# Attention in halves of the heads, a hand-ordered first group, and unread products on TensorE

## The chip, the cores and the metric

One core of a Trainium2 chip. The metric is device microseconds (us) of one execution; a median is over the executions of a kernel that were timed. The trace's span (first to last instruction) is 1.8 to 2.2 us shorter than the timed figure. All runs told of here are in the fast state. Times inside a kernel are us from the span's start.

Some words used throughout: a *turn* is a transposition on TensorE; *kv*, *q_t*, *product* and *turn* are the steps of attention, and a *leftover* step does the same for the 64 leftover tokens of two batches; the *chain* is the work followed back from the last instruction, at each step to what released it; the *granted clock* is the share of full speed that TensorE was allowed, and half rate is 0.5.

## The reference, cut to what matters

```python
# q, k, v: (8, 8, 576, 64) fp32
kv  = einsum('bhsd,bhse->bhde', k, v)
out = einsum('bhsd,bhde->bhse', q, kv)
out = out / sqrt(mean(out*out, -1) + 1e-6) * g_norm
x = out as (4608, 512)                 # tokens by heads*dim
y = ((x @ w1) * (x @ w2) @ w3) @ w_out # d_ff 1024, weights in fp64
```

The kernel folds w3 and w_out into one matrix (`w3o`, the fold stage), and works on nine groups T of 512 tokens: one for 512 tokens of each of the 8 batches, and a last one (`x_left`) for the 64 leftover tokens of all batches. A group has a gate stage (x @ w1, x @ w2 and their product, 8 column blocks f) and a projection by `w3o`. The attention of batch T+1 is put in pieces between the gate blocks of group T. The weights arrive as 8 byte words, 512 KB for a piece, and are converted to fp32 on ScalarE and VectorE.

## The kernel before

```python
w1_sb = const.tile([P, NP, DF], FP32, name="w1_sb")     # 128 x 4 x 1024
w2_sb = const.tile([P, NP, DF], FP32, name="w2_sb")

def load_raw(src):                      # 512 KB of 8 byte words
    raw = fold.tile([P, c, n], src.dtype, name="raw", bufs=4)
    nc.sync.dma_start(out=raw, in_=src)

def convert(dst, raw):                  # ScalarE: low, abs; VectorE: four steps
    nc.scalar.activation(low, lo, AF.Copy, ...)              # L116
    nc.scalar.activation(dst, hi.bitcast(FP32), AF.Abs)      # L117
    nc.vector.tensor_scalar(out=dst, ...)                    # L118
    nc.vector.tensor_scalar(out=dst_bits, ...)               # L121
    nc.vector.scalar_tensor_tensor(out=low_bits, in0=hi, ..) # L124, last to read raw
    nc.vector.tensor_tensor(out=dst_bits, ..., op=ALU.add)   # L128

def gate(T, f):
    cols = slice(f * P, (f + 1) * P)
    for w_sb in (w1_sb, w2_sb):
        g_ps = bank(ps_mm, "mm")
        for c in range(NP):
            nc.tensor.matmul(g_ps, lhsT=w_sb[:, c, cols], rhs=xT[T][:, c, :], ...)
    nc.scalar.copy(a_sb, prods[0])
    nc.vector.tensor_mul(ab[T, f], a_sb, prods[1])
# ... (cut: kv, q_t, product, norm, turn of attention)
# first group
load_batch(0)
for f, piece in enumerate(attention(0)):
    raws = [load_raw(gate_src(w, f)) for w in (w1, w2)]
    for w_sb, raw in zip((w1_sb, w2_sb), raws):
        convert(w_sb[:, :, f * P:(f + 1) * P], raw)
    piece()
# ... (cut)
for T in range(NG):
    pieces = attention(T + 1) if T + 1 < B else []
    late = 3 if T == 0 else 0
    for f in range(KF):
        gate(T, f)
        due = max(f + 1 - late, 0) * len(pieces) // (KF - late)
        # T == 0: load and convert part f of w_out; then run pieces[done:due]
    # T == 0: turn w3 and fold it with w_out
    project(T)
```

TensorE's order is the program's; that of the other engines is chosen by a scheduler.

## Time and profile before

| | before |
|---|---|
| median | 971.7 us (3 runs, 970.5 to 972.5) |
| span of the profiled run | 969.7 us |
| first gate in full swing | 64.0 |
| first fold block | 144.3 |
| project(0) starts | 206.2 |
| after that | 763.5 us with no wait of TensorE |

The page, the waits, the stretches and the chain are shown and read in the prediction below. One thing that it passed over is in the timeline of TensorE before (start us, duration us, engine, line, operation, tile written <- read, shapes, count, idle before and its releaser):

```profile
49.93 2.08 PE L292 MATMUL mm<-xT,w_sb 128*128 128x512 f32 x2 [0.78 <-ACT xT L263]
64.00 6.16 PE L292 MATMUL mm<-xT,w_sb 128*128 128x512 f32 x8 [11.99 <-DVE w_sb L128]
```

The first gate issues two instructions (one of its eight products; an fp32 product is two instructions), stands 12 us and then goes on. Its own column block had been converted by then: with a tile of its own this gate runs through from 49.2 (before_wtiles, below). What it stood for is the subject of half of the experiments.

### The profile page before, as it was taken

How to read it: one execution, taken by the hardware profiler on the slowest of the kernel's cores; microseconds unless marked ns; L12 is line 12 of the kernel's file. 1: busy time of each engine (PE TensorE's matmuls, PEld its weight loads, DVE VectorE, ACT ScalarE, POOL GpSimd, SP SyncE). 2: the span in 40 equal slices, each digit the busy share in tenths (PEclk: the TensorE clock that was granted, in tenths of full speed). 3: DMA queues.
4: the chain of work that ended last, by engine and by line, in shares of the span. 5: the costliest groups of instructions: out<-in, count | busy, mean ns of one | idle time of the engine just before them, and what ended most of it. 6: DMA issues, size and time to landing. Idle time of an engine off the chain costs nothing.

```text
span 969.7 us, 7839 instructions
## 1 busy us (share of the span) xinstructions
PE 915.6 (94%) x3232; PEld 455.6 (47%) x3232; DVE 223.8 (23%) x421; ACT 182.1 (19%) x332; POOL 0.7 (0%) x6
## 2 busy tenths in 40 slices
PE   4249979999999999999999999999999999999998
PEld 4214554444554455445544554554455544444443
DVE  2986256600120122112201220122012200000010
ACT  2663243300121022102200220122012200000000
POOL 0000000000000000000000000000000000000000
PEclk9659999999999999999999999999999999999999
DMA  8984413100310131013003200310000000000001
GB/s 233 279 276 156 141 55 130 44 11 33 98 44 19 36 96 45 22 53 93 18 22 98 65 12 22 112 51 1 32 11 1 1 33 11 0 22 22 1 0 43
DMA packets 54980, 59.23 MB, mean 61 GB/s; under 512 B 14496, under 2 KB 47264, under 8 KB 54944
## 3 DMA queue, kind: packets, MB, share of 16 engines
q1 hardware_dynamic: 54944, 58.73, 19.7%
q8 instruction: 25, 0.41, 0.2%
q14 instruction: 11, 0.09, 0.0%
HBM read 49.28 MB, written 9.44 MB: 61 GB/s over the span
## 4 chain that ended last, share of the span: by engine, by line
PE 93%; DVE 3%; DMA 2%; ACT 1%; issue 1%; SPq 0%; DVEq 0%; ACTq 0%
PE mm L292 51%; PE mm L344 25%; PE mm L333 6%; PE at L163 3%; PE at L223 3%; PE at L258 1%; PE at L180 1%; DMA v_sb<-in_v_dram 1%; DMA raw<-in_moe_w_dram 1%; DVE low L124 1%; PE mm L316 1%; DVE w_sb L128 1%; PE at L244 1%; ACT low L116 0%; DVE w_sb L118 0%
## 5 line engine op out<-in xcount | busy, mean ns | idle before, releaser
L292 PE MATMUL mm<-xT,w_sb 128*128 128x512 f32 x1024 | 453.2, 597 | 12.8 <-DVE w_sb L128 12.0
L292 PEld LDWEIGHTS mm<-xT,w_sb 128*128 128x128 f32 x1024 | 191.9, 191 | 238.9 <-issue 223.0
L344 PE MATMUL mm<-w3o_sb,ab 128*128 128x512 f32 x576 | 248.7, 592 | 0.0
L344 PEld LDWEIGHTS mm<-w3o_sb,ab 128*128 128x128 f32 x576 | 109.0, 190 | 134.9 <-issue 134.7
L303 DVE TENSOR_TENSOR ab<-a_sb,mm 128x512 f32<-128x512 f32 x72 | 49.5, 688 | 435.9 <-PE mm L292 435.9
L301 ACT COPY a_sb<-mm 128x512 f32<-128x512 f32 x72 | 42.2, 586 | 275.5 <-PE mm L292 275.5
L352 ACT COPY o_sb<-mm 128x512 f32<-128x512 f32 x18 | 10.5, 586 | 256.2 <-PE mm L344 256.2
L333 PE MATMUL mm<-wo_sb,w3T 128*128 128x512 f32 x128 | 57.7, 606 | 0.0
L292 PE MATMUL mm<-x_left,w_sb 128*128 128x512 f32 x128 | 55.1, 592 | 0.0
L354 DVE COPY o_sb<-mm 128x512 f32<-128x512 f32 x18 | 12.5, 692 | 176.4 <-PE mm L344 176.4
L258 PE MATMUL at<-ident,xn 128*128 128x128 f32 x144 | 23.7, 293 | 20.6 <-DVE xn L210 20.6
L223 PEld LDWEIGHTS at<-kv_bd,qT 128*128 128x128 f32 x256 | 34.8, 200 | 15.0 <-issue 12.4
L200 ACT ACTIVATE sq<-at 128x512 f32<-128x512 f32 (+1 forms) x40 | 22.1, 551 | 102.0 <-PE at L223 101.0
L292 PEld LDWEIGHTS mm<-x_left,w_sb 128*128 128x128 f32 x128 | 24.3, 190 | 30.6 <-issue 30.6
L333 PEld LDWEIGHTS mm<-wo_sb,w3T 128*128 128x128 f32 x128 | 24.5, 196 | 28.3 <-issue 28.0
L223 PE MATMUL at<-kv_bd,qT 128*128 128x128 f32 x256 | 35.9, 286 | 1.6 <-DVE xn L210 1.0
L163 PE MATMUL at<-v_sb,k_sb 128*64 128x64 f32 x512 | 23.7, 240 | 11.6 <-DMA v_sb<-in_v_dram 11.6
L202 DVE TENSOR_REDUCE inv<-sq 128x8 f32<-128x512 f32 (+1 forms) x40 | 25.3, 632 | 30.5 <-ACT sq L200 30.5
L258 PEld LDWEIGHTS at<-ident,xn 128*128 128x128 f32 x144 | 18.3, 150 | 28.8 <-DVE xn L210 12.2
L116 ACT ACTIVATE low<-raw 128x512 f32<-128x512 uint32 x40 | 27.0, 676 | 20.7 <-DVE w_sb L128 17.8
L263 ACT ACTIVATE xT<-at,g_col 128x512 f32<-128x512 f32 x32 | 21.9, 685 | 47.7 <-PE at L258 47.7
L124 DVE SCALAR_TENSOR_TENSOR low<-raw,low 128x512 uint32<-128x512 uint32 x40 | 27.1, 687 | 7.5 <-ACT low L116 6.9
(39 smaller groups left out, 295.4 us busy)
## 6 DMA issues: line engine op xcount, KB each, us to landing
raw<-in_moe_w_dram SPq DMA_DIRECT2D x32, 512.0 KB, 4.5
k_sb<-in_k_dram SPq DMA_DIRECT2D x8, 1024.0 KB, 6.0
v_sb<-in_v_dram SPq DMA_DIRECT2D x8, 1024.0 KB, 8.9
q_sb<-in_q_dram SPq DMA_DIRECT2D x8, 1024.0 KB, 5.3
out_dram<-o_sb SPq DMA_DIRECT2D x32, 256.0 KB, 2.3
raw<-in_moe_w_out_dram SPq DMA_DIRECT2D x8, 512.0 KB, 4.1
kl_sb<-in_k_dram SPq DMA_DIRECT2D x8, 128.0 KB, 6.2
vl_sb<-in_v_dram SPq DMA_DIRECT2D x8, 128.0 KB, 8.8
```

The costliest lines, as they stand in the source:

```text
L116: nc.scalar.activation(low, lo, AF.Copy, scale=2.0 ** -51, bias=2.0)
L124: nc.vector.scalar_tensor_tensor(out=low_bits, in0=hi, scalar=0x80000000, in1=low_bits, op0=ALU.bitwise_and, op1=ALU.bitwise_or,)
L163: nc.tensor.matmul(kv_ps[e * D:(e + 1) * D, r, :], lhsT=k_sb[:, h, cols] if j < J else kl_sb[:, h, :], rhs=v_sb[:, h, cols] if j < J else ...
L200: nc.scalar.activation(sq[:, cols], o_ps[:, cols], AF.Square)
L202: nc.vector.tensor_reduce(out=inv, in_=sq[:, cols].rearrange("p (h d) -> p h d", d=D), axis=AX.X, op=ALU.add,)
L223: nc.tensor.matmul(o_ps[:, h * P:(h + 1) * P], lhsT=qT[i, half][:, h, :], rhs=bd[:, half * HB + h, :], start=True, stop=True,)
L258: nc.tensor.transpose(t_ps[:, r, :], xn[:, 2 * r:2 * r + 2, :], ident)
L292: nc.tensor.matmul(g_ps, lhsT=w_sb[:, c, cols], rhs=xT[T][:, c, :], start=(c == 0), stop=(c == NP - 1),)
L301: nc.scalar.copy(a_sb, prods[0])
L303: nc.vector.tensor_mul(ab[T, f], a_sb, prods[1])
L333: nc.tensor.matmul(f_ps, lhsT=t[:, j, :], rhs=wo_sb[:, j, :], start=(j == 0), stop=(j == KF - 1))
L344: nc.tensor.matmul(o_ps, lhsT=ab[T, f][:, m * P:(m + 1) * P], rhs=w3o_sb[:, f, :], start=(f == 0), stop=(f == KF - 1),)
```

## The change

Its intent: start TensorE earlier. Batch 0 is loaded and worked on in two halves of the heads; the first group's work on ScalarE, VectorE and the load queue is put in program order, with the weights of gate f+2 converted before gate f; w_out and the first w3 pieces ride along; batch 1's attention moves into the fold stage; and 24 products that nobody reads keep TensorE's clock up in the early waits. The core of the diff:

```diff
-    def load_batch(b):
+    def load_half(b, half):            # k, kl, v, vl, q of four heads
+        heads = slice(half * HB, (half + 1) * HB)
...
+        pieces = []
+        for half in range(2):
+            pieces += [
+                [(kv, half), (q_t, 0, half)],
+                [(product, 0, half), (q_t, 1, half)],
+                [(product, 1, half), (turn, 0, half)],
+                [(turn, 1, half)],
+            ]
+        if b % 2:
+            pieces[6] += [(q_t_left,)]
+            pieces[7] += [(product_left,)]
+            pieces += [[(turn_left,)]]
...
+    def keep_warm(n):
+        t = bank(ps_mm, "mm")
+        for _ in range(n):
+            nc.tensor.matmul(t[:, 0:P], lhsT=ident, rhs=ident, start=True, stop=True)
...
+        keep_warm(16)
+        for name in ("kv0", "q_t00", "q_t10", "product00", "product10"):
+            first[name]()
+        keep_warm(4)
+        # ... second half, convert_gates(0), keep_warm(4), turns, convert_gates(1)
+        for f in range(KF):
+            wo_raw = load_wo(f)
+            if f + 2 < KF:
+                raws = load_gates(f + 2)
+                convert_gates(f + 2, raws)
+            else:
+                i = f + 2 - KF
+                w3_sb[i] = convert_w3(load_w3(i))
+            convert(wo_sb[:, f:f + 1, :], wo_raw)
+            gate(0, f)
+            if f in (3, 5):
+                load_half(1, f // 4)
...
+    for i in range(KF):                # fold stage, with batch 1's pieces
+        ...
+        pieces[i]()
+        fold_block(i)
+    pieces[KF]()
...
+    for T in range(1, NG):
+        # ...
+            due = (f + 1) * len(pieces) // KF
```

Also: copies of kv split between VectorE and ScalarE, one buffer fewer for `ab` and `o_sb` each, and one more for `qT`. In the changed kernel the conversion's lines are L130, L131 (ScalarE) and L132, L135, L138, L142 (VectorE), the gate's matmul is L322 and its product L333, the w3 turn L351, the fold L368, the projection L379, the leftover product L256, its transpose L282, the unread products L412.

> **What bounds the kernel now.** I read the page's busy shares and slices first, to see which engine is the limit and where it isn't.
>
> ```profile
> PE 915.6 (94%) x3232; PEld 455.6 (47%) x3232; DVE 223.8 (23%) x421; ACT 182.1 (19%) x332; POOL 0.7 (0%) x6
> ...
> PE   4249979999999999999999999999999999999998
> ...
> PEclk9659999999999999999999999999999999999999
> ```
>
> TensorE is the limit, and every hole in it lies in the first six slices of 24.2 us. Nothing can be won after 145 us, only lost. The waits of TensorE over the whole span say the same (engine, line, what it waited for, us in total, times, longest):
>
> ```profile
> PE at L258 <- DVE xn L210: 20.6, 4, 8.9
> PE mm L292 <- DVE w_sb L128: 12.0, 1, 12.0
> PE at L163 <- DMA v_sb<-in_v_dram: 11.6, 1, 11.6
> ...
> ```
>
> So: 11.6 us until batch 0 has landed; 20.6 us of transposes waiting for a norm; 12.0 us of the first gate waiting for converted weights. Asked for the waits after 206 us, the trace has none by a matmul. Busy times by stretch then show how bad the start is (us, busy time and count of PE, PEld, DVE, ACT, POOL, then granted clock, DMA share, GB/s):
>
> ```profile
> 40.00:50.00 10.00, 1.61 (x7) 1.21 (x7) 7.53 (x16) 4.03 (x7) 0.00 (x0) 0.50 1.12 285
> 50.00:60.00 10.00, 2.01 (x2) 0.43 (x2) 6.84 (x14) 5.00 (x9) 0.00 (x0) 0.50 0.95 302
> 130.00:140.00 10.00, 7.55 (x58) 5.50 (x56) 3.41 (x9) 3.87 (x8) 0.00 (x0) 0.86 0.00 1
> 140.00:150.00 10.00, 7.06 (x19) 3.50 (x19) 8.72 (x17) 5.71 (x9) 0.00 (x0) 0.80 0.63 211
> ```
>
> Last, the chain that ended last gives the stages (start us, us, what):
>
> ```profile
> 64.00 29.34 PE mm L292 x62
> ...
> 132.80 0.91 PE at L244 x19
> ...
> 136.74 0.43 DVE xn L210
> 137.31 1.09 PE at L258 x4
> ...
> 206.24 18.88 PE mm L344 x44
> ```
>
> The gates of group 0 run steadily from 64.0, batch 1's attention is spread among them, the fold of w3 with w_out takes over at 138, and project(0) begins at 206.2. From there 763.5 us of dense TensorE work remain. The change can win in the 206 us before that point. The middle lines show a cost I need below: the leftover product (L244) is followed at once by its own transpose (L258), and TensorE stands for the norm between them.
>
> **What the Trainium skill says.** (1) "TensorE: Matmul & The Clock Gate", Part 1: The HAM clock gate: the array is half-rate by default and a free-running window of 3413 ns decides. The trace agrees: from windows of 0.5 and 1 us the clock falls at 28.0, 137.25 and 144.1; 109.2 us is 32 such windows, 6.85 is two. (2) Same page, "Why this matters for your kernels": no idle gaps over some 3 us. Here 2.45 us (134.85 to 137.31) was enough, and the clock was half until 140.6. (3) Same page, "Architectural detail": ScalarE and VectorE are strict FIFO. That matters as the change fixes their program order. (4) "DMA: Bandwidth & Descriptors", "Anatomy of one DMA": about 2.0 us fixed plus the bytes, stated for another descriptor path. Here a 512 KB piece takes at least 3.0 us to land (last row of the next fences), so a load issued only when its data are due costs about that much.
>
> **The change part by part.**
>
> *Unit costs.* A gate block is 16 matmul instructions in 6.87 us (chain rows "6.87 PE mm L292 x16"); a fold block the same; one w3 turn of a row block 0.87; batch 1's attention: 3.51 kv, 1.76 q transposes, 3.56 products, 0.44 + 1.5 leftovers, 1.76 + 0.44 turns, 13 us. A conversion, from the timeline (start us, us, ...):
>
> ```profile
> 59.80 0.42 DVE L118 TENSOR_SCALAR w_sb<-w_sb 128x512 f32<-128x512 f32 x1
> 60.25 0.43 DVE L121 TENSOR_SCALAR w_sb<-w_sb 128x512 uint32<-128x512 uint32 x1
> 60.62 0.69 DVE L124 SCALAR_TENSOR_TENSOR low<-raw,low 128x512 uint32<-128x512 uint32 x1
> 61.23 0.68 DVE L128 CUSTOM_DVE_ANT_0 w_sb<-w_sb,low 128x1024 uint16<-128x1024 uint16 x1
> 61.83 0.42 DVE L118 TENSOR_SCALAR w_sb<-w_sb 128x512 f32<-128x512 f32 x1
> ```
>
> and the loads of such pieces, from the view of that buffer:
>
> ```profile
> DMA to landing us min/median/max: 3.0/4.4/8.7
> ```
>
> That is 2.0 us of VectorE per raw piece of 512 KB, after 1.35 us of ScalarE (L116, L117); the raw buffer is free when L124 ends, 1.44 us into it.
>
> *Start, by halves.* The first kv needs 1.18 MB in place of 2.36. At the 0.29 MB/us of the first 20 us, from 1.9 us, plus the 2 us by which the old landing (11.5) exceeds that reckoning: 7.9 us. The unread products (32 instructions) warm the array before. Half 1's v lands near 13.3. Following the norm through ScalarE and VectorE in order (square 0.6, sum 0.69, root 0.3, reciprocal 0.2, product 0.69) the last norm ends near 23; the four gate pieces 0 and 1 convert at 23.3 to 31.3. The first gate starts near 27 rather than 64.
>
> *Gate stage.* Per block VectorE has three conversions and one product, 3 x 2.0 + 0.65 = 6.7 us, against 6.87 of TensorE, which looks balanced. But the raw ring has still 4 buffers, and pieces are now loaded in the order w_out(f), gate a(f+2), gate b(f+2) and converted a, b, w_out. Numbering the loads, a(f+2) takes the buffer of w_out(f-1), the last converted before it, and is itself the next due. So every block pays a whole load: 3.2 us landing (estimate from the 3.0 minimum) + 1.35 ScalarE + 2.0 + 2.0 + 1.44 until w_out releases its buffer = 10.0 us. Block 0 releases at 31.4 + 5.44 = 36.8; seven more give 107; the two halves of batch 1 pushed into the queue at f = 3 and 5 (1.77 MB each, 6 us) add about 1 each: 109, and 110 with the last L128. TensorE's gates (6.87 of 10 us) hide under this, cold or not.
>
> *Fold stage.* The first fold needs all of w_out, hence the 110, and turn 1 and the first attention piece at half clock (some 5 us from 107.8) make it 112.5. Then 8 x 6.87 + 6 x 0.87 + 10.5 of attention = 70.7. The old wait for the leftover norm is gone here, a fold block lies between. project(0) starts near 184 instead of 206.2: 22 us won, of a possible 43 if the gate stage ran at TensorE's pace.
>
> *The later groups.* Odd batches now have nine pieces over eight gates, so (f+1) x 9 // 8 gives seven pieces by f = 6 and two after f = 7: turn and leftover product, and at once the leftover turn. Before, a gate lay between:
>
> ```profile
> 385.72 1.47 PE at L244 x32
> 387.19 7.06 PE mm L292 x16
> 394.26 0.87 PE at L258 x8
> ```
>
> In groups 2, 4 and 6 (batches 3, 5, 7) TensorE therefore stands as it did at 134: leftover product from 132.73 to 134.27, turn at 137.31, 3.0 us. The clock probably falls for one window: half of 3.4 is 1.7, times a chance I put at 0.7 from how the gap falls across windows: 1.2. Three times 4.2 = 12.7 us lost. The copies of kv moved to ScalarE, a smaller o_sb and ab ring and the split turns lie under 6.87 us gates and cost nothing.
>
> *Sum:* 969.7 - 22 + 12.7 = 960 of span, and 1.8 for the usual difference to the timed figure: **962 us**, 1.0% faster.
>
> **The rivals.** *A: the ring doesn't stall.* If loads run far enough ahead, the gate stage is 8 x 6.9 and fold starts some 22 us earlier: 940. For it: VectorE and DMA have the throughput (285 to 302 GB/s above, 12.6 MB + 3.5 in 55 us). Against: four buffers and this order. *B: the leftover wait is short or filled.* Then about 950 with the stall, 928 without. Against: 3.0 us measured in the same situation. *C: the start is DMA bound.* The stage needs 16 MB, 55 us at 0.29 MB/us; as each block also waits, more contention than my 2 us could make the stage 10 us longer: 972. *D: halves stall the later groups,* as loads of T+2 wait for halves of T+1. Against: 12 us of loads, and 27 us of project(T) plus the last gates to hide them in; I give it nothing.
>
> **Range and chances.** The sum has eight times the uncertainty of a load's latency (0.5 us each: 4 us), 3 us in the start, 4 us in the leftover waits. Around 962 that is some 6 us; A and B give a tail below. 80%: 944 to 970. Over 2% faster is under 952.3: both stalls as sized, 0.70, with a 0.04 chance of it; only the ring, 0.12 at half; only the leftovers, 0.13 at 0.9; neither, 0.05: together 0.26. Slower by 2%: 0.02. Within: 0.72.
>
> **What would show it.** First kv near 8 and first gate near 27. Gate stage: conversions in bursts of three with a VectorE hole of about 3 us each 10 us, put down to the raw load; with period near 7 the ring step is wrong. First fold near 112, project(0) near 184. In groups 2, 4 and 6, about 3 us of transpose waiting for xn each; none anywhere else after project(0). If idle of TensorE appears in odd groups at their start, D is right; if project(0) starts before 170 or the leftover waits are under 1 us, the prediction is too slow.

## The result, and the profile after

968.6 us median of 4 runs (967.75 to 969.64) against 972.0 (970.5 to 972.54) of the kernel before on the same chip. The ratio is 0.9968, 95% interval 0.9951 to 0.9985. Ratios here are the mean time of one kernel's fast runs over that of the kernel before in the same rounds, so they are not quite the ratio of the medians quoted. The gain is 0.3%, where 1.0% was forecast.

The changed kernel's page (busy time and share; then the slices, now of 24.1 us):

```profile
PE 927.7 (96%) x3280; PEld 460.0 (48%) x3280; DVE 222.1 (23%) x421; ACT 189.8 (20%) x364; POOL 0.7 (0%) x6
...
PE   8588999999999998999999989999999899999998
...
PEclk9789999999999998999999989999999899999999
```

The first slices are far fuller. But there are three new dents, in slices 16, 24 and 32, in both PE and clock: they come every two groups. TensorE's waits in it:

```profile
PE mm L322 <- DVE w_sb L142: 18.7, 7, 6.4
PE at L282 <- DVE xn L226: 8.9, 3, 3.0
PE at L271 <- DVE xn L226: 1.4, 1, 1.4
```

The wait for batch 0 has gone from 11.6 us to 0.2 beside the unread products, and that for norms at the start from 20.6 to some 2. The gates still wait 18.7 us for conversions. The leftover transposes (L282) wait three times 3.0. The chain that ended last, at the stages that matter:

```profile
36.00 8.39 PE mm L322 x14
44.48 0.69 DVE ab L333
45.17 0.35 DVE w_sb L132
...
46.60 0.70 DVE w_sb L142
47.35 6.29 PE mm L322 x14
...
113.52 6.87 PE mm L368 x16
...
184.79 27.47 PE mm L379 x64
```

Project(0) starts at 184.8, where 184 was forecast: 21.4 us won (206.24 - 184.79). From there on the changed kernel needs 780.8 us (965.6 - 184.8), the kernel before 763.5: 17.3 us given back. What is left of the span is 4.1.

The chain also shows what happens at a leftover transpose (group 2):

```profile
375.67 0.43 DVE xn L226
376.10 0.14 issue
376.24 1.09 PE at L282 x4
377.32 29.65 PE mm L379 x64
```

The transposes take 1.09 us where four of them took 0.44 before, and the projection 29.65 where it takes 27.47. The stretches behind it (us, busy of PE, PEld, DVE, ACT, POOL, granted clock, DMA share, GB/s) say why:

```profile
374.50:378.00 3.50, 1.76 (x6) 1.28 (x7) 1.12 (x4) 0.94 (x2) 0.00 (x0) 0.54 0.00 0
378.00:381.50 3.50, 3.50 (x6) 1.43 (x5) 0.00 (x0) 0.05 (x1) 0.00 (x0) 0.50 0.00 0
381.50:385.00 3.50, 3.50 (x10) 1.59 (x9) 0.00 (x0) 0.00 (x0) 0.00 (x0) 0.99 0.00 0
```

The array is at half rate for 6.83 us, from 374.8 to 381.6 (edges worked out from the mean clock of stretches of 0.25 us), and it is so at all three such places of this run. This place costs 3.0 of waiting, 0.65 on the transposes and 2.18 on the projection: 5.8. At the other two the projection loses 2.10 and 2.06, and the three come to 17.2. That is the 17.3.

And the gate stage, in TensorE's timeline and in that of the load queue (SPq: the issue of a load):

```profile
27.50 2.07 PE L322 MATMUL mm<-xT,w_sb 128*128 128x512 f32 x2 [1.66 <-DVE w_sb L142]
36.00 9.23 PE L322 MATMUL mm<-xT,w_sb 128*128 128x512 f32 x16 [6.43 <-DVE w_sb L142]
```

```profile
34.54 0.68 DVE L138 SCALAR_TENSOR_TENSOR low<-raw,low 128x512 uint32<-128x512 uint32 x1
35.29 2.48 SPq L118 DMA_DIRECT2D raw<-in_moe_w_dram  x2
```

The same signature as before the change: two instructions, then a stand until 36.0, which is the end of the fifth conversion on VectorE, that is of gate a of block **2**, though this is gate 0. In the chain every block up to the sixth waits so: 14 of its 16 instructions start when a conversion for two blocks on has ended. VectorE in turn stands before the product (`ab`) until the gate is done; it waited so six times, 20.3 us in all. The second fence refutes my reading of the raw ring: the next load of gate pieces goes out at 35.29, just as the L138 of a gate piece has ended, 4 us before w_out's own L138 (38.79 to 39.47) has released its buffer. So the buffers here are handed out by the order of their release in the program, not in turn.

### The profile page after: what moved, and what is told of

The parts are those of the page before. It is cut to its first block, busy times and chain, and to the rows that moved or that the text cites. A ratio compares the mean times of both kernels' runs of the same rounds, so it can differ in the third digit from the quotient of the medians.

```text
span 965.6 us, 8046 instructions
## 1 busy us (share of the span) xinstructions
PE 927.7 (96%) x3280; PEld 460.0 (48%) x3280; DVE 222.1 (23%) x421; ACT 189.8 (20%) x364; POOL 0.7 (0%) x6
## 4 chain that ended last, share of the span: by engine, by line
PE 94%; DVE 4%; ACT 1%; DMA 1%; issue 0%; SPq 0%; DVEq 0%; ACTq 0%
PE mm L322 52%; PE mm L379 26%; PE mm L368 6%; PE at L239 3%; PE at L176 3%; PE at L198 1%; PE at L271 1%; PE mm L351 1%; DVE w_sb L142 1%; DVE low L138 1%; DMA v_sb<-in_v_dram 1%; DVE inv L218 1%; DVE w_sb L135 0%; PE at L256 0%; DVE xn L226 0%
## 5 line engine op out<-in xcount | busy, mean ns | idle before, releaser
L322 PE MATMUL mm<-xT,w_sb 128*128 128x512 f32 x1024 | 457.6, 602 | 18.7 <-DVE w_sb L142 18.7
L322 PEld LDWEIGHTS mm<-xT,w_sb 128*128 128x128 f32 x1024 | 193.5, 193 | 250.6 <-issue 225.5
L379 PE MATMUL mm<-w3o_sb,ab 128*128 128x512 f32 x576 | 255.2, 604 | 0.0
L379 PEld LDWEIGHTS mm<-w3o_sb,ab 128*128 128x128 f32 x576 | 111.5, 195 | 138.6 <-issue 138.6
L333 DVE TENSOR_TENSOR ab<-a_sb,mm 128x512 f32<-128x512 f32 x72 | 49.5, 687 | 446.5 <-PE mm L322 446.5
L368 PE MATMUL mm<-wo_sb,w3T 128*128 128x512 f32 x128 | 56.4, 593 | 0.0
L322 PE MATMUL mm<-x_left,w_sb 128*128 128x512 f32 x128 | 55.1, 592 | 0.0
L322 PEld LDWEIGHTS mm<-x_left,w_sb 128*128 128x128 f32 x128 | 24.3, 190 | 30.6 <-issue 30.6
L368 PEld LDWEIGHTS mm<-wo_sb,w3T 128*128 128x128 f32 x128 | 23.7, 190 | 26.9 <-issue 26.5
L239 PE MATMUL at<-kv_bd,qT 128*128 128x128 f32 x256 | 33.8, 276 | 0.9 <-ACT qT L200 0.9
L130 ACT ACTIVATE low<-raw 128x512 f32<-128x512 uint32 x40 | 27.2, 679 | 37.8 <-DVE w_sb L142 27.6
L200 ACT COPY qT<-at 128x512 f32<-128x512 f32 x32 | 18.5, 585 | 63.0 <-PE at L198 62.9
L138 DVE SCALAR_TENSOR_TENSOR low<-raw,low 128x512 uint32<-128x512 uint32 x40 | 27.2, 684 | 1.0 <-ACT low L130 0.7
L226 DVE TENSOR_TENSOR xn<-at,inv 128x512 f32<-128x512 f32 (+1 forms) x40 | 25.5, 638 | 4.3 <-DVE inv L225 0.5
L131 ACT ACTIVATE w_sb<-raw 128x512 f32<-128x512 f32 x32 | 21.2, 670 | 7.9 <-PE mm L351 7.9
```

The lines of the kernel that those rows point to most:

```text
L130: nc.scalar.activation(low, lo, AF.Copy, scale=2.0 ** -51, bias=2.0)
L138: nc.vector.scalar_tensor_tensor(out=low_bits, in0=hi, scalar=0x80000000, in1=low_bits, op0=ALU.bitwise_and, op1=ALU.bitwise_or,)
L226: nc.vector.tensor_tensor(out=dst, in0=o_ps[:, cols].rearrange("p (n m d) -> p n m d", m=m, d=D), in1=inv.rearrange("p (n m) -> p n m", m= ...
L239: nc.tensor.matmul(o_ps[:, h * P:(h + 1) * P], lhsT=qT[i, half][:, h, :], rhs=bd[:, half * HB + h, :], start=True, stop=True,)
L368: nc.tensor.matmul(f_ps, lhsT=t[:, j, :], rhs=wo_sb[:, j, :], start=(j == 0), stop=(j == KF - 1))
L379: nc.tensor.matmul(o_ps, lhsT=ab[T, f][:, m * P:(m + 1) * P], rhs=w3o_sb[:, f, :], start=(f == 0), stop=(f == KF - 1),)
```

## The experiments

Two losses had to be explained: the gate stage with 10.35 us a block ((87.73 - 36.00) / 5 from the chain) rather than 6.9, and the 17.3 us behind project(0).

- Theory *shared tile*: the gate waits for conversions of later blocks because the program tracks what a write touches by an address range. Row c of w1's block f lies at elements 1024c + 128f; the conversion of block f+2 spans 128(f+2) to 3072 + 128(f+3), and rows 1 to 3 of block f lie within it. Row 0 doesn't, and those are the two instructions that pass.
- Rival *raw ring*, of my prediction: a load is issued only when its data are due.
- Theory *leftover*: three waits with their clock. Rival: the halves themselves cost the later groups something.

| run | edit to the changed kernel | median us | ratio | first fold | project(0) |
|---|---|---|---|---|---|
| changed kernel | | 968.6 | 0.9968 | 113.4 | 184.6 |
| wtiles | a tile per column block | 954.6 | 0.983 | 100.5 | 173.7 |
| blockmajor | one tile, laid out by blocks | 954.9 | 0.9818 | 101.1 | 173.6 |
| loadorder | w_out loaded after the gate pieces | 961.5 | 0.9917 | 112.7 | 183.9 |
| left1 | leftover steps one piece earlier | 952.0 | 0.9804 | 114.4 | 186.2 |
| leftfill | 13 unread products in the wait | 960.6 | 0.9888 | 114.4 | 185.7 |
| again | nothing | 967.0 | 0.9943 | 114.6 | 185.8 |
| nowarm | no unread products | 967.4 | 0.9968 | 114.3 | 185.6 |
| both | wtiles and left1 | 941.4 | 0.9689 | 101.1 | 174.8 |
| bothlate | and batch 1's half later | 937.0 | 0.9643 | 96.9 | 168.5 |
| best2 | see below | 938.5 | 0.9657 | 88.3 | 170.9 |
| best3 | see below | 931.0 | 0.9577 | 89.1 | 164.8 |
| before_wtiles | a tile per column block, in the kernel **before** | 957.0 | 0.9849 | 131.1 | 192.7 |

The last two columns are the first instruction of the stage in TensorE's timeline (us); the chain's figures lie some 0.2 later. All outputs were correct; all had 3 rounds (again: 5). The runs lay on several chips; the kernel before, run in the same rounds, had medians from 970.4 to 972.2.

### The gate stage

**wtiles**

```diff
-    w1_sb = const.tile([P, NP, DF], FP32, name="w1_sb")
+    w1_sb = [const.tile([P, NP, P], FP32, name=f"w1_sb{f}") for f in range(KF)]
     # w2_sb likewise
-                    lhsT=w_sb[:, c, cols],
+                    lhsT=w_sb[f][:, c, :],
-            convert(w_sb[:, :, f * P:(f + 1) * P], raw)
+            convert(w_sb[f], raw)
```

> The changed kernel with each of the 8 column blocks of w1 and w2 in a tile of its own. Theory 'shared tile': gate(0,f) stood for the conversion of block f+2 only because w1_sb and w2_sb are one tile each, whose rows c = 1 to 3 of block f lie inside the address range that the conversion of block f+2 writes. Then group 0's gates start at their own weights, first fold near 92 us in place of 113.5, total near 947. Theory 'raw ring' of the prediction: no change, 968.6, first fold near 113.

TensorE's timeline of this run has the gates in one piece from 27 us on:

```profile
27.16 20.21 PE L322 MATMUL mm<-xT,w_sb 128*128 128x512 f32 x40 [1.66 <-DVE w_sb L142]
```

The gates' wait for conversions fell from 18.7 us to 1.7, in the list of TensorE's waits:

```profile
PE mm L322 <- DVE w_sb L142: 1.7, 1, 1.7
```

The theory holds. But the gain was 14 us, not 22, and the first fold came at 100.5, not 92: with the false wait gone, a true one shows. Its chain has, in the gate stage:

```profile
55.86 7.45 DMA raw<-in_moe_w_dram
68.33 3.49 DMA raw<-in_moe_w_dram
73.19 7.12 DMA raw<-in_moe_w_dram
85.33 6.12 DMA raw<-in_moe_w_dram
```

Two of these loads stand in the queue behind a half of batch 1, issued at 51.4 and 68.8. My rival A (stage at TensorE's pace, 940) had left that out.

**blockmajor**

```diff
-    w1_sb = const.tile([P, NP, DF], FP32, name="w1_sb")
+    w1_sb = const.tile([P, KF, NP, P], FP32, name="w1_sb")
     # w2_sb likewise
-                    lhsT=w_sb[:, c, cols],
+                    lhsT=w_sb[:, f, c, :],
-            convert(w_sb[:, :, f * P:(f + 1) * P], raw)
+            convert(w_sb[:, f], raw)
```

> The changed kernel with w1 and w2 still one tile each, but laid out block by block, so that the bytes of one column block are one stretch. Theory 'address range': the false wait came from the spread-out rows of a block reaching over the next ones, so this does as well as separate tiles: first fold near 101 us, 954.6 (less where the clock windows fall better at the leftover waits). Rival 'whole tile': the wait is for any write to the tile, nothing changes: first fold near 113, 968.6.

954.9 us: the same tile, laid out so that a block's bytes are one stretch, does as well as eight tiles. So it is the range, not the tile.

**loadorder**

```diff
         for f in range(KF):
-            wo_raw = load_wo(f)
             if f + 2 < KF:
                 # load and convert the gate pieces
...
-            convert(wo_sb[:, f:f + 1, :], wo_raw)
+            convert(wo_sb[:, f:f + 1, :], load_wo(f))
```

> The changed kernel with the raw pieces loaded in the order in which they are converted (w_out(f) after the gate pieces). Theory 'raw ring' of the prediction: the stall of a whole load per block goes, period 7 us, total near 947. Theory 'shared tile': the period stays near 10.3 us, 968.6 within noise.

The first fold moved by 0.7 us (112.7 for 113.4) and the gates wait as before:

```profile
PE mm L322 <- DVE w_sb L142: 18.7, 7, 6.4
```

The raw ring as I had it is dead. Still the time fell by 7 us, which neither theory had. Of the 6.7 us that the span lost, 6.1 lie behind project(0), where nothing had been edited: 774.9 us for 781.0 from the first instruction of project(0) on. The next part explains it.

**before_wtiles** (the diff of wtiles, on the kernel before)

> The kernel before with each column block of w1 and w2 in its own tile and nothing else. Theory: its first gate too stood at 49.9 us after one of its four row blocks, until 64.0, for the conversion of the last column block; with tiles of their own the gates run from 50 on as far as the weights are converted: 8 to 12 us less, 960 to 964. Rival (the weights' arrival is the bound there): under 4 us, 968 or more.

957.0: some 14 us less than the kernel before, where 8 to 12 were expected. Its chain runs gates from 49.2 us on:

```profile
49.18 0.04 issue
49.23 30.78 PE mm L292 x64
```

So the false wait was in the kernel before as well, there for the conversion of the very last block. Two edited declarations and their uses give the kernel before more (1.5%) than the whole change (0.3%).

### Behind project(0)

**left1**

```diff
         if b % 2:
-            pieces[6] += [(q_t_left,)]
-            pieces[7] += [(product_left,)]
-            pieces += [[(turn_left,)]]
+            pieces[5] += [(q_t_left,)]
+            pieces[6] += [(product_left,)]
+            pieces[7] += [(turn_left,)]
```

> The changed kernel with the leftover steps one piece earlier, so that a gate block lies between the leftover product and its transpose. Theory: the three waits of 3.0 us and the half clock after them go, 3 x 5.8 = 17.5 us: 951. Rival (the later groups lose by the halved kv and turns instead): at most a few us, 965 or more.

952.0. Its chain in group 2, to be set against the four lines of the changed kernel above:

```profile
366.03 1.85 PE at L256 x32
367.88 7.06 PE mm L322 x16
374.94 0.44 PE at L271 x4
375.38 0.44 PE at L282 x4
```

A gate lies between product and transpose, nothing is waited for, and no stretch around the three places shows a lowered clock. From project(0) to the end it takes 765.5 us, against 763.6 of the kernel before measured alike. Of these 1.8 us, 1.1 belong to left1's own order: its leftover product takes 1.85 us three times, where the kernel before has 1.47. That leaves some 0.7 us that the halves and the moved copies can have cost the later groups, and the rival falls.

**leftfill**

```diff
-            for piece in pieces[done:due]:
-                piece()
+            for i in range(done, due):
+                if i == KF:
+                    keep_warm(13)
+                pieces[i]()
```

> The changed kernel with 13 unread products (some 2.9 us) ahead of the leftover transpose in groups 2, 4 and 6: the wait for the norm stays as long, only the clock is kept. Theory 'two half-rate windows each': granted clock stays 1.0 after the wait, 3 x 2.8 = 8.4 us saved, 960. If the clock costs what the prediction said (1.2 each): 965. If it costs nothing: 968.6 or a little more.

960.6, as the theory had it. The chain:

```profile
372.90 1.47 PE at L256 x32
374.37 3.10 PE mm L412 x26
377.47 0.50 PE at L282 x4
377.97 2.15 PE mm L379 x5
```

The wait is still there, filled with 3.1 us of unread products, and the clock was full at all three places. So some half of the 17.2 was waiting (8.9), the other half clock (8.3). This is the one place where these runs show unread products to earn anything.

**again** (no edit)

> The changed kernel, nothing altered, profiled once more. Theory 'window lottery': the three leftover waits stay 3.0 us each, but which of the free-running 3.41 us windows go to half rate depends on where they fall, so this profile may show another edge phase and another cost after the waits (0 to 2.8 us each), and the times may spread from 960 to 970. If the cost is a fixed property of the kernel: half rate for 6.8 us at each of the three again, all times within 967 to 970.

The six times spread from 961.15 to 969.09, those of the first four runs from 967.75 to 969.64. In this profile each of the three waits was followed or accompanied by 3.41 us at half rate, not 6.83, with the waits as long as ever. In loadorder it was 0, 3.41 and 0 us. The stretches of loadorder and of this run that begin at 374.50, to be set against the 0.54 above (the clock is the third figure from the end):

```profile
374.50:378.00 3.50, 2.45 (x9) 1.45 (x10) 0.60 (x2) 0.85 (x2) 0.00 (x0) 1.00 0.00 0
374.50:378.00 3.50, 0.58 (x3) 0.61 (x4) 1.84 (x6) 0.87 (x3) 0.00 (x0) 0.82 0.00 0
```

The other profiles with these waits had 6.83 at each (wtiles), 3.41, 6.83 and 6.83 (blockmajor), 3.41, 3.41 and 0 (nowarm). The clock's edges within one run lie whole numbers of 3.413 us windows apart (among the falls, 26.61, 57.33 and 88.05 in the changed kernel and 25.61, 56.33 and 87.05 in loadorder: nine windows each time), but the offset differs from run to run. So the cost of a leftover wait is a lottery over where it falls in the windows: up to 2.8 us, when two windows are lost. In the profiled run the three places are 194.71 and 194.64 us apart, 57.0 windows, so all three fell alike. That distance contains the clock's own cost and is no constant of the kernel: in loadorder it was 192.1 and 193.8. The lottery accounts for most of loadorder's 7 us as well. Which share of a window has to be busy isn't settled: the window before the fall in the changed kernel held 1.5 us of waiting, with transposes and leftover products of quarter size in nearly all the rest; one of loadorder after which it didn't fall held about 1.8 us of waiting and 1.2 us of dense matmuls. How much each kind of work counts was not tried.

**nowarm** (all three calls of `keep_warm` taken out)

> The changed kernel without its 24 unread products. Theory: they only keep the array warm before the first kv, and the chain there then waits for the second half of batch 0 (v lands near 13 us), so at most 1.5 us: 967 to 970. If they carried the gain, as the name of the change suggests: the first kv, transposes and products at half rate, some 4 us or more: 973 or above.

967.4, beside 967.0 of the unaltered kernel in the same rounds. The first kv is indeed slower, 3.02 us for 40 instructions in place of 1.85, and it is made up for before the first fold (114.3, again: 114.6). The unread products bring nothing to the changed kernel that these runs can see; whether they would in a kernel without the false wait was not tried.

### Towards a better kernel

**both** (diffs of wtiles and left1)

> Separate tiles for the column blocks and the leftover steps one piece earlier. Theory: the two losses are independent and add: 954.6 - 17.5 = 937, no wait of TensorE after project(0) begins. If they overlap: 945 or more.

941.4. In spans the step from wtiles is 14.5 us (954.7 to 940.2): 15.5 behind project(0), as much as left1 won there (781.0 to 765.5), less 1.1 before it. So the two losses add. Of the 2 us that are missing to the expectation's 17.5, 1.1 are the slower leftover product of left1's order (1.85 for 1.47, three times).

**bothlate** (on top of both)

```diff
-            if f in (3, 5):
-                load_half(1, f // 4)
-        load_left(1)
+            if f == 5:
+                load_half(1, 0)
+        load_half(1, 1)
+        load_left(1)
```

> As the one before, and the second half of batch 1 loaded after the gate stage, the first at f = 5 alone. Theory: with the false wait gone the gate stage is bound by raw pieces that queue behind batch 1's 1.77 MB halves (7 us holes after f = 3 and 5); one of the holes goes: first fold near 95 in place of 101, 931. Rival: the depth of four raw buffers is the bound by itself: first fold stays near 100, 937.

937.0, which is the rival's figure; but the first fold came 4.2 us earlier (96.9), where the theory had 6 and the rival almost nothing. VectorE is busy 9.3 to 9.7 of every 10 us from 25 to 75 us, so four raw buffers alone don't bind there. The conversions go on almost without a hole until the half at f = 5, which still costs one (7.0 of 10 us from 75 to 85). How much of the 6 us missing to 931 that hole makes was not tried alone: best2 changes the buffers and the loads together.

**best2** (wtiles, left1, loadorder; five raw buffers, paid for with one buffer of qT and one of ab; both halves of batch 1 after the gate stage; each attention piece behind its fold block)

> What the runs point to: own tiles for the column blocks, leftover steps one piece earlier, gate pieces loaded ahead of w_out's, five raw buffers (one qT and one ab buffer fewer), both halves of batch 1 loaded after the gate stage, and each attention piece behind its fold block. Theory: the gate stage is then bound by VectorE alone, 28 conversions of 2.12 us and 8 products of 0.69 from 25.4 us on: first fold near 91, project(0) near 165, 931. If loads still bind: 935 or more.

The first half of the expectation came true (first fold at 88.3), the time did not: 938.5. Two w3 pieces for the second turn had queued behind both halves of batch 1, and TensorE stood from 97 to 104 for all but 2.4 us of work, then folded its second block partly at half rate (8.67 us for 6.87).

**best3** (the other parts of best2, in it too, are left out here)

```diff
-            if f in (3, 5):
-                load_half(1, f // 4)
-        load_left(1)
+        load_half(1, 0)
...
     for i in range(KF):
         # ... convert_w3, turn_w3
-        pieces[i]()
+        if i == 1:
+            load_half(1, 1)
+            load_left(1)
         fold_block(i)
+        pieces[i]()
```

> As best2, but only the first half of batch 1 is loaded right after the gate stage, the second behind the w3 pieces of fold blocks 2 and 3. In best2 the first fold came at 88.5 as expected, but the w3 pieces for the next turn queued 6 us behind both halves of batch 1, so TensorE stood and cooled there. Theory: that hole goes, project(0) near 164 in place of 171, 931. If it is something else: 937 to 939 as before.

931.0 us (930.21 to 932.13), 4.2% below the kernel before. Its longest waits of TensorE:

```profile
PE mm L351 <- DVE w_sb L142: 2.5, 1, 2.5
PE mm L322 <- DVE w_sb L142: 1.7, 1, 1.7
PE at L271 <- DVE xn L226: 1.4, 1, 1.4
```

The gate stage is now bound by VectorE, above all by its conversions: VectorE is busy 9.5 to 9.7 of every 10 us from 25 to 85, and the first fold comes at 89, where 91 was reckoned from VectorE's work alone.

## Why the prediction was right or wrong

The time, 962 forecast and 968.6 measured, lies in the stated range of 944 to 970. The gain was forecast at 1.0% and measured at 0.3%. Two steps of the prediction failed: the mechanism of the gate stage, at no cost to the sum, and the size of the clock's loss in the later groups, which made the gap.

- *Start by halves.* Right: first kv at 7.67 (7.9), the first gate instruction at 27.5 (27).
- *Gate stage.* The size is right, the mechanism wrong. The failed step is "a(f+2) takes the buffer of w_out(f-1), the last converted before it, and is itself the next due. So every block pays a whole load". It doesn't take that buffer, and loadorder, which undoes the order, changed nothing there. In its place stands a false dependence of gate f on the conversion of block f+2: conversion of one gate piece (2.1), then the gate (6.3 to 8.4 by the clock), then the product (0.7), each waiting for the other. That this sums to the 10 us of my wrong sum is chance. The sign that I had named came out half: VectorE does work in bursts of three with a hole (up to 4.3 us), but the hole ends with the gate, not with a load. I had both signs of the false wait before me: the wait of 12 us for a conversion, and the two instructions ahead of it, and I read the first as a wait for the gate's own weights.
- *Fold stage.* Right: first fold 113.5 (112.5), project(0) 184.8 (184), 21.4 us won (22).
- *The later groups.* The mechanism is right, and left1 shows it: three waits, 3.0 us each, in groups 2, 4 and 6, and nothing else. The term that was off is "The clock probably falls for one window: half of 3.4 is 1.7, times a chance I put at 0.7 from how the gap falls across windows: 1.2". It measured 2.7 to 2.8 (0.65, and 2.06 to 2.18) at each of the three, two windows rather than 0.7 of one: the wait of 3.0 us lay half in the window before the fall and half in the next, and the clock stayed low after both. In all the three places cost 17.2 us and not 12.7, 4.5 more. The gap between the forecast's 9.3 us of span (22 less 12.7) and the measured 4.1 is 5.2; the first part's 0.6 makes up nearly all the rest. Part of this is bad luck: the unaltered kernel ran from 961.15 to 969.09 in again, where the waits cost one window each in the profile, so 962 lies within what the windows' offset alone does. What the prediction lacked is the second window, and that the three can fall alike.
- *Rivals.* A was the right suspicion for the wrong reason, and 940 was too good: wtiles made 954.6, as loads then bind. B is what left1 did: 952, where I had said about 950. C and D did not come about.
- *Small slips.* By the prediction's own lines a raw buffer is free 1.51 us into a conversion (59.80 to 61.31), not 1.44, and 112.5 and 70.7 make 183.2, not 184; nothing hangs on either. That ScalarE and VectorE keep strict order, its third point from the skill, no run tested by itself.

## What to carry to other kernels

When a matmul starts, issues one slice and then stands for a conversion of data that it doesn't use, look at how the tiles are laid out: give each block that is written on its own a tile or a contiguous stretch of its own. When a piece list doesn't divide evenly over the slots, see which producer and consumer end up back to back at the seam: here TensorE paid for the wait (3.0 us) and then for its clock (0 to 2.8 us). A change that wins 21 us at the start may give back 17 in places that repeat, so compare what is left after the last edited stage before looking at details.

## What the Trainium skill lacked or had wrong

- "TensorE: Matmul & The Clock Gate", "Why this matters for your kernels" advises against idle gaps of more than some 3 us. Here waits of 3.0 us, each with transposes and quarter-size products ahead of it, cost 0, 3.4 or 6.8 us at half rate by where they fell in the free-running window, and one of 2.45 us cost 3.4. The page doesn't say that one gap can spoil two windows.
- The same page, Part 1, puts the penalty of the ramp under 1% of a typical span. The three leftover waits alone cost 8.3 of 965.6 us in clock, 0.9%, so it holds, but that is twice what the change gained. The page has nothing on gaps that repeat at a whole number of windows: the three of the profiled run (194.7 us, 57.0 windows apart) fell alike. Two profiles of one kernel had 6.83 and 3.41 us at half rate at each of the three.
- The same page warns that recorded clock events can be unreliable, and names a clock stuck low; it doesn't name a start without a record. Here the stretch from 8 to 11 us of nowarm reads 1.00 though its first record lies at 15.1, while the first kv took 3.02 us there and 1.85 with unread products, which speaks for a slow clock.
- No page has it that a program's dependence tracking can let a strided write hold up readers of other parts of the tile, by its address range. Here that cost some 14 us in either kernel (wtiles, before_wtiles).
- No page says in which order buffers of a tile ring are handed out. Here it was the order of release, 4 us ahead of what taking turns would have given.
